# Seven products instead of eight for two token blocks in the second expert chunk, with its token sums and gate steps moved

## The chip, the cores and the metric

The kernel runs on one core of a Trainium2 chip. The metric is device time in microseconds (us), from launch to end, as the median of several executions. The core's engines are TensorE (PE, with its weight loads as PEld), VectorE (DVE), ScalarE (ACT) and GpSimd (POOL); SyncE (SP) issues DMAs. Each engine works through its own queue in order, and semaphores make an instruction wait for others.

## The reference

Three stages follow each other, on 2 x 768 = 1536 tokens of 512 values: windowed attention with 4 sink positions (8 heads of 64), a mixture of 8 experts whose gate is normalized 8 times over rows and columns, and one wide feed-forward layer with a squared ReLU.

```python
x = attention(q, k, v)                      # keep: sink or 0 <= rel < window
logits = x @ w_gate; P = exp(logits - logits.max())
for _ in range(8):
    P /= P.sum(1, keepdims=True) + 1e-09
    P /= P.sum(0, keepdims=True) + 1e-09
    P *= N / E
for e in range(E):
    out += P[:, e:e+1] * (np.maximum(x @ w1[e], 0.0) @ w2[e])
return (np.maximum(out @ w_in, 0.0) ** 2) @ w_out
```

## The kernel before

**Precision and products.** Every float32 operand is kept as two float32r tiles, a rounded high part and the rest (xh and xl, w2h and w2l, hh and hl). ACT writes the high part, and POOL or DVE subtracts it to get the rest. A float32 product is three products on PE: high by rest, high by high, rest by high. `pair_split` (L480 to L482) is the ACT copy and the POOL subtraction of weights and token sums.

**Chunks.** The hidden dimension is cut into chunks of 512: 16 for the experts (two for each expert), 4 for the last layer. Chunk 0 is worked on while attention runs: its groups (`first_groups`) fill PE between attention's steps, in token blocks of 384 (`mm1`, `mm2`). What is left of them when attention ends is drained at the head of `phase_b`, and three second groups of its last block (`rest`) are carried into chunk 1, the second chunk. From chunk 1 on the tokens are in three blocks of 512, numbered 0, 1 and 2.

**First products.** `plain` takes 12 PE products of 512 columns for 128 hidden values of one block. So two blocks need 8 groups, 96 products. The fast chunks (2 to 15, and later 17 to 19) take blocks 0 and 1 together by the seven-product scheme for 2 x 2 blocks: `fast` builds 14 groups of 6 products, 84 in all, for the two halves of the chunk. Each half has five sums out of PSUM on DVE (`tt`, L822), one copy on ACT (L836) and four results, of which each is rounded by ACT and then reduced to hl by DVE (`to_h`, L730 and L740). A set of seven uses four PSUM banks (a, b, c, d); the product p3 writes again to bank c after e5 has read it, p4 to bank d after e7.

**Operands of the scheme.** Weight sums S1 to S4 come from POOL (`unit_sums`, L525, four subtractions of 128x256 per half) and are split by `units`. Token sums T1 to T4 come from `sums` (L671 to L714): differences on DVE (L683) in the scratch tiles x0, x2 and u, then `pair_split`. T1 is written over block B12 of xh and xl (values 0 to 255 of tokens 512 to 1023), so after that block 1 can't be used plain, nor by the gate. T2 to T4 lie in tiles of their own. `sums(0)` is for blocks 0 and 1, with 512 columns, `sums(1)` for the halves of block 2, with 256. Both are planned into chunk 1.

**Second products.** `second` takes 12 products for 128 tokens (L913), and DVE adds the result into acc (`add_up`, L646 in chunk 1). In chunk 2 acc is first scaled by P (L649), from then on every sum is weighted by P (L653).

**The gate.** `gate` (L946) is a generator. Its first three steps are 8 products each (L953, zero-padded gate weights wgz by all tokens of a block) with a copy on ACT; the fourth transposes and takes the maximum per partition; the fifth takes the maximum over partitions (L979) and negates it (L980); the sixth spreads it by a PE product (L983), takes the exponential, and starts the rounds. A round is a PE product with a matrix of ones for the column sums (L1001), a reciprocal and a scaling on DVE (L1005, L1006), and the next row sums, reciprocals, scaling and column sums (L990, L991, L992, L995). P must be ready for chunk 2's sums.

**Order.** It is written out by hand. `run` issues the groups of a list one after the other; behind group k come the steps that `put` has planned for k; and when the running number of the group (from 0 at the head of chunk 1) is in GATE_AT, the next gate step. The PSUM tile of a group is one of 8 banks in turn. DMAs of weights are issued by SP in the order of `load_list`, into three buffers: the fourth is asked for when the first has been used.

Chunk 1 before: one plain group of block 1, three carried-over groups, 7 plain groups of blocks 1 and 0, 4 second groups of block 1, 4 plain groups of block 2, 8 second groups of blocks 0 and 2. The sums for blocks 0 and 1 are behind the groups 0 to 12 of the last 23 of these, those for block 2 behind the groups 15 to 21. The gate's steps begin with the first group and end in chunk 2.

Of the kernel before, what the change touches and what calls it, by code (L numbers as in the profile page):

```python
# [37 lines left out]
NC = NC1 + NC2  # L38
CONV = 3
CONV_AT = (0, 1, 2, 3, 8, 9, 10, 11, 12, 13, 14, 15)  # L40
GATE_AT = (0, 1, 2, 3, 5, 7, 9, 11, 13, 16, 19, 22, 25, 30)
W2_AT = (2, 5, 8, 11)
NB = 512
BIG = 1e30
# [4 lines left out]
class Kernel:  # L49
# [30 lines left out]
    def masks_begin(self):  # L80

        nc, c = self.nc, self.const
        self.raw_nw = self.att.tile([1, 4], I32, name="nw_i")
        for k, src in enumerate((self.nsink, self.window)):
            nc.scalar.dma_start(out=self.raw_nw[:, 2 * k : 2 * k + 2], in_=src.bitcast(I32))
        self.row = self.acc[0:1, NTILE - 1, 0:128]
        nc.vector.memset(self.row, 1.0)
        warm = self.att.tile([128, 1], F32, name="warm")
        nc.vector.memset(warm, 0.0)
        nc.scalar.activation(out=warm, in_=warm, func=AF.Exp)  # L90
        di, ci = self.scratch(0).bitcast(I32), self.scratch(1).bitcast(I32)
        nc.gpsimd.iota(di, pattern=[[-1, 256]], base=128, channel_multiplier=1)
        nc.gpsimd.iota(ci, pattern=[[1, 256]], base=0, channel_multiplier=0)
        nc.vector.tensor_copy(out=self.scratch(2), in_=di)
        self.pm = self.ps_xs.tile([128, 512], F32, tag="xs", name="pm")
        nc.vector.tensor_copy(out=self.pm[:, 256:512], in_=ci)
        nc.vector.tensor_scalar(
            out=self.pm[:, 0:256], in0=self.scratch(2), scalar1=0.0, scalar2=None, op0=ALU.is_lt
        )
        self.ident = c.tile([128, 128], F32, name="ident")  # L100
        make_identity(nc, self.ident)
        a = self.att
        self.junk = a.tile([128, 1], F32, name="junk")
# [332 lines left out]
    def load_list(self, c0):  # L436

        loads, k = [(c0, which, half) for which in range(2) for half in range(2)], 0
        for c in range(c0, NC):
            wide = [(j, 2, 0) for j in range(k, min(k + CONV, 8 * NC2)) if c >= 2]  # L440
            k += len(wide)
            n = c + 1
            loads += wide[0:1]
            if n < NC:
                if self.is_fast(n):
                    loads += [(n, 3, 0), (n, 3, 1)]
                loads += wide[1:2] + [(n, 0, 0)] + wide[2:3] + [(n, 0, 1), (n, 1, 0), (n, 1, 1)]
            else:
                assert len(wide) < 2
        return loads  # L450
# [217 lines left out]
        o = 2 * NB * q + w * t  # L668
        return tuple(x[:, k : k + 2, o : o + w] for x in (self.xh, self.xl))

    def sums(self, q):  # L671

        nc = self.nc
        T = [
            self.tp.tile([128, 3, 2, NB >> q], F32R, tag=f"T{q}{t}", name=f"T{q}{t}")
            for t in "hl"
        ]
        self.T[q] = T

        def tt(o, a, b, op):  # L680
            if isinstance(o, str):
                o = self.scratch2(o)[:, 0 : NB >> q]
            nc.vector.tensor_tensor(out=o, in0=a, in1=b, op=op)  # L683
            return o

        B = {n: self.operand(n, q) for n in ("B11", "B12", "B21", "B22")}
        f32 = lambda n, hl, kc: B[n][hl].bitcast(F32)[:, kc]

        def put(name, kc, x):
            hi, lo = self.operand(name, q)  # L690
            self.pair_split(hi[:, kc], lo[:, kc], x)

        for kc in range(2):
            x = tt("x0", f32("B22", 0, kc), f32("B12", 0, kc), ALU.subtract)
            y = tt("u", f32("B22", 1, kc), f32("B12", 1, kc), ALU.subtract)
            yield
            t3 = tt("x2", x, y, ALU.add)
            put("T3", kc, t3)
            yield
        for kc in range(2):  # L700
            x = tt("x0", f32("B12", 0, kc), f32("B11", 0, kc), ALU.subtract)
            y = tt("u", f32("B12", 1, kc), f32("B11", 1, kc), ALU.subtract)
# [196 lines left out]
    def second(self, c, t):  # L899

        def group(k):
            def go():
# [4 lines left out]
                for i in range(cuts):  # L907
                    d = slice(DM // cuts * i, DM // cuts * (i + 1))
                    ps = self.mmtile()
                    n = 0  # L910
                    for f in (0, 1, 3, 2):
                        for x, w in ((hh, wh), (hh, wl), (hl, wh)):
                            self.nc.tensor.matmul(  # L913
                                out=ps[:, d], lhsT=x[:, f, s], rhs=w[:, f, d], start=(n == 0),
# [127 lines left out]
    def run(self):  # L1042
# [18 lines left out]
        if True:  # L1061
            with tc.manual_schedule():
                first = ExitStack()
                self.wp = self.pool(first, "wp0")
                self.hp0 = self.pool(first, "hp0")
                with ExitStack() as actx:
                    self.wraw = self.pool(actx, "wraw0")
                    self.att = self.pool(actx, "att")
# [124 lines left out]
    def phase_a(self, gen):  # L1193
# [16 lines left out]
        self.att_load_v(1)  # L1210
        for n in (HP - 1, HP):
            self.att_load_qk(n)
        fill = self.filler(gen)
        at = next(fill)
        for u in range(U + 2):
# [56 lines left out]
                self.w_load(0, 1)  # L1272
            if u == 20:
                self.general_flag()
        return fill

    def phase_b(self, c0, first, fill):

# [17 lines left out]
        ]  # L1296
        self.loads, self.lk, self.used = self.load_list(c0), 0, set()
        self.next_loads()
        self.wgz = self.xp_.tile([128, KD, 128], F32R, tag="x0", name="wgz")
        wgr = self.xp_.tile([128, KD, E], F32, tag="x2", name="wgr")  # L1300
        nc.gpsimd.memset(self.wgz.bitcast(F32), 0.0)
        self.ones = self.xp_.tile([128, 128], F32, tag="x1", name="ones")
        nc.gpsimd.memset(self.ones, 1.0)
        nc.sync.dma_start(out=wgr, in_=self.wg)
        todo = [partial(self.units, c0, half, 0, k) for half in range(2) for k in range(2)]
        for _ in fill:
            if self.done:
                self.evac()
                if todo:
                    todo.pop(0)()  # L1310
        self.evac()
        for step in todo:
            step()
        hz = self.wgz[:, :, 0:E]
        nc.scalar.activation(out=hz, in_=wgr, func=AF.Copy)
        nc.vector.tensor_tensor(
            out=self.wgz[:, :, E : 2 * E], in0=wgr, in1=hz.bitcast(F32), op=ALU.subtract
        )
        gate = self.gate()
        groups = itertools.count()  # L1320

        def run(seq, plan):

            for k, g in enumerate(seq):
                g()
                for step in plan.get(k, ()):
                    step()
                if next(groups) in GATE_AT:
                    next(gate, None)

        conv = itertools.chain.from_iterable(self.wide(k) for k in range(8 * NC2))
# [3 lines left out]
        for c in range(c0, NC):  # L1335
# [6 lines left out]

            off = 0
            if not low:
                run([self.plain(c, 1, 0), *rest], {})
                low = first.close() or True
                self.w2p = self.pool(left, "w2" + n)
                self.tp = self.pool(left, "T" + n)
                self.cp, self.T = self.pool(left, "c" + n), {}
                seq = [self.plain(c, t, f) for t in (1, 0) for f in range(KD)][1:]  # L1350
            elif self.is_fast(c):
                seq = self.fast(c, 0, 0) + self.fast(c, 1, 0)
            else:
                seq = [self.plain(c, t, f) for t in (1, 0) for f in range(KD)]
            for k in range(4):
                put(W2_AT[k] if self.is_fast(c) else k, self.part_w2, c, k)
            if c == NC1:
                x = [self.x2(2, kc) for kc in range(KD)]
                seq = sum(([s, *x[k : k + 1]] for k, s in enumerate(seq)), [])
            m = len(seq)  # L1360
            if self.is_fast(c):
                (a, b, *e), (f, g, *i) = (self.fast(c, half, 1) for half in range(2))
                if c < FAST2:
                    seq += self.second(c, 1) + [a, b, f, g]
# [11 lines left out]
            if c == NC1 - 1:  # L1376
# [2 lines left out]
                    ([s, x[k]] for k, s in enumerate(self.second(c, 0) + self.second(c, 2))), []  # L1379
                )  # L1380
                wide = lambda k: m + k if k < 8 else m + 2 * k - 8
            else:
                seq += self.second(c, 0) + self.second(c, 2)
                wide = lambda k: m + k
            if c in (FAST - 1, FAST2 - 1):
                t = self.sums(0)
                for k in range(13):
                    put(k if c < FAST else min(2 * k, k + 5), next, t, None)
                t = self.sums(1)
                for k in range(13):  # L1390
                    put(m + 8 + k // 2, next, t, None)
            if c + 1 < NC:
                if self.is_fast(c + 1):
                    for half in range(2):
# [105 lines left out]
```

## Time and profile before

| | us |
|---|---|
| median of 3 runs (lowest, highest) | 1379.7 (1379.4, 1380.33) |
| the profiled execution's own time | 1379.64 |
| its span, first to last instruction | 1377.8 |
| PE busy in the span | 1363.2 (99%) |
| DVE busy | 955.4 (69%) |
| POOL busy | 501.3 (36%) |
| ACT busy | 453.1 (33%) |

The span is the time from the first to the last instruction; the execution's own time is 1.84 us longer. A share of busy time is a mean over stages that are limited by different engines. The second chunk lies at 181.7 to 247.35 us of the span, behind the fill and the three carried-over groups (from 152 us on).

### The profile page before, as it was taken

What the parts mean: (1) busy time and instruction counts of PE and PEld (TensorE: products, weight loads), DVE (VectorE), ACT (ScalarE), POOL (GpSimd) and SP (SyncE); (2) the same over time, 40 slices, a digit from 0 to 9 for tenths busy, and PEclk for the clock granted to TensorE, in tenths of its full rate; (3) what the DMA queues carried; (4) which work ended last, traced back from release to release, by engine and by line L of the source; (5) the groups of instructions that cost most, each with busy time, mean ns of one, the idle gap of its engine ahead of it and who ended that gap; (6) DMA issues with size and microseconds to landing.
All of it is one profiled execution on the core that took longest, in us unless ns stands there. A gap on an engine that the chain in (4) does not pass through costs nothing.

```text
span 1377.8 us, 18905 instructions
## 1 busy us (share of the span) xinstructions
PE 1363.2 (99%) x7105; PEld 1141.7 (83%) x7105; DVE 955.4 (69%) x1884; ACT 453.1 (33%) x1007; POOL 501.3 (36%) x442
## 2 busy tenths in 40 slices
PE   8999999999999999999999999999999999999998
PEld 5677888888888888888888888888888888888887
DVE  8777369887777777777777768765454568866564
ACT  6776322322232222222232222222232243433331
POOL 4322136524343434424343434423343036543210
PEclk9999999999999999999999999999999999999999
DMA  5222200132313232232313232230102010111101
GB/s 203 81 90 73 78 31 31 62 94 73 124 54 109 79 96 85 92 107 67 118 54 122 70 95 82 92 107 32 61 32 77 16 62 16 62 55 54 46 24 72
DMA packets 61147, 102.53 MB, mean 74 GB/s; under 512 B 3957, under 2 KB 43253, under 8 KB 60789
## 3 DMA queue, kind: packets, MB, share of 16 engines
q1 hardware_dynamic: 61040, 101.22, 23.2%
q8 instruction: 58, 0.95, 0.3%
q14 instruction: 45, 0.36, 0.1%
q10 hardware_dynamic: 4, 0.00, 0.0%
HBM read 89.67 MB, written 11.53 MB: 73 GB/s over the span
## 4 chain that ended last, share of the span: by engine, by line
PE 79%; DVE 1%; ACT 0%; issue 0%; DVEq 0%; ACTq 0%
PE mm L913 42%; PE mm L762 36%; PE mm L930 0%; ACT tx L733 0%; DVE acc L653 0%; DVE tx L734 0%; ACT hh L745 0%; DVE tx L822 0%; DVE hl L746 0%; DVE acc L649 0%; DVE mm L734 0%; DVE raw L578 0%; ACT tx L836 0%; DVE tu L822 0%; DVE raw L565 0%
## 5 line engine op out<-in xcount | busy, mean ns | idle before, releaser
L913 PE MATMUL mm<-w2h,hh 128*128 128x512 f32 (+1 forms) x916 | 357.0, 390 | 0.0
L913 PE MATMUL mm<-w2l,hh 128*128 128x512 f32 (+1 forms) x916 | 355.9, 388 | 0.0
L913 PE MATMUL mm<-w2h,hl 128*128 128x512 f32 (+1 forms) x916 | 355.6, 388 | 0.0
L482 POOL TENSOR_TENSOR w2l<-raw,w2h 128x512 fp32r<-128x512 f32 x76 | 118.5, 1559 | 365.7 <-ACT w2h L481 363.7
L653 DVE SCALAR_TENSOR_TENSOR acc<-mm,P,acc 128x512 f32<-128x512 f32 x168 | 125.7, 748 | 135.6 <-PE mm L913 134.4
L913 PEld LDWEIGHTS mm<-w2h,hl 128*128 128x128 f32 x916 | 172.0, 188 | 35.8
L913 PEld LDWEIGHTS mm<-w2h,hh 128*128 128x128 f32 x916 | 172.1, 188 | 34.6
L913 PEld LDWEIGHTS mm<-w2l,hh 128*128 128x128 f32 x916 | 172.1, 188 | 34.3
L525 POOL TENSOR_TENSOR raw<-raw 128x256 f32<-128x256 f32 x136 | 125.1, 923 | 7.9
L482 POOL TENSOR_TENSOR s0l<-raw,s0h 128x512 fp32r<-128x512 f32 (+1 forms) x36 | 45.5, 1264 | 198.6 <-ACT s0h L481 198.6
L730 ACT ACTIVATE hh<-tx 128x512 fp32r<-128x512 f32 (+1 forms) x112 | 58.8, 525 | 130.0 <-DVE tx L822 129.5
L822 DVE TENSOR_TENSOR tx<-mm,tu 128x512 f32<-128x512 f32 (+1 forms) x136 | 75.6, 556 | 20.9 <-PE mm L762 16.6
L822 DVE TENSOR_TENSOR tx<-mm,tx 128x512 f32<-128x512 f32 (+1 forms) x68 | 37.9, 557 | 57.8 <-PE mm L762 56.5
L740 DVE SCALAR_TENSOR_TENSOR hl<-tx,hh 128x512 fp32r<-128x512 f32 (+1 forms) x112 | 70.1, 626 | 9.7 <-ACT hh L730 9.6
L836 ACT ACTIVATE tx<-mm 128x512 f32<-128x512 f32 x34 | 20.3, 598 | 154.9 <-PE mm L762 153.0
L646 DVE TENSOR_TENSOR acc<-mm,acc 128x512 f32<-128x512 f32 (+1 forms) x49 | 33.2, 677 | 48.2 <-PE mm L913 47.9
L730 ACT ACTIVATE hh<-mm 128x512 fp32r<-128x512 f32 (+1 forms) x68 | 34.0, 501 | 99.2 <-PE mm L762 99.2
L836 ACT ACTIVATE txs<-mm 128x256 f32<-128x256 f32 x34 | 13.0, 381 | 151.3 <-PE mm L762 151.3
L482 POOL TENSOR_TENSOR a0l<-raw,a0h 128x512 fp32r<-128x512 f32 (+1 forms) x38 | 43.0, 1148 | 51.5 <-ACT a0h L481 47.5
L762 PE MATMUL mm<-xl,a1h 128*128 128x512 f32 (+1 forms) x172 | 60.3, 350 | 0.2 <-ACT tx L836 0.2
L762 PE MATMUL mm<-xl,a0h 128*128 128x512 f32 (+1 forms) x172 | 59.8, 348 | 0.0
L762 PE MATMUL mm<-xh,a0h 128*128 128x512 f32 (+1 forms) x172 | 59.8, 347 | 0.0
(262 smaller groups left out, 3149.5 us busy)
## 6 DMA issues: line engine op xcount, KB each, us to landing
raw<-w SPq DMA_DIRECT2D x110, 512.0 KB, 3.7
raw<-win SPq DMA_DIRECT2D x16, 512.0 KB, 4.0
w<-m SPq DMA_DIRECT2D x32, 256.0 KB, 4.6
raw<-wout SPq DMA_DIRECT2D x16, 512.0 KB, 4.0
raw<-qkv SPq DMA_DIRECT2D x8, 624.0 KB, 5.0
raw<-qkv SPq DMA_DIRECT2D x7, 464.0 KB, 3.9
out<-acc SPq DMA_DIRECT2D x11, 256.0 KB, 2.0
wraw<-w SPq DMA_DIRECT2D x2, 1024.0 KB, 6.7
```

The source lines that it names most:

```text
L482: self.nc.gpsimd.tensor_tensor(out=lo, in0=src, in1=hi.bitcast(F32), op=ALU.subtract)
L525: self.nc.gpsimd.tensor_tensor(out=o, in0=x, in1=y, op=op)
L646: nc.vector.tensor_tensor(out=a, in0=ps, in1=a, op=ALU.add)
L653: nc.vector.scalar_tensor_tensor(out=a, in0=ps, scalar=self.P[:, ti, e : e + 1], in1=a, op0=ALU.mult, op1=ALU.add)
L730: nc.scalar.activation(out=hh, in_=src, func=AF.Relu)
L740: nc.vector.scalar_tensor_tensor(out=hl, in0=src, scalar=0.0, in1=hh.bitcast(F32), op0=ALU.max, op1=ALU.subtract,)
L762: self.nc.tensor.matmul(out=ps, lhsT=w[:, kc], rhs=x[:, kc], start=start and k == 0, stop=(k == n - 1), skip_group_check=True,)
L822: nc.vector.tensor_tensor(out=v[name], in0=v[a], in1=v[b], op=ALU.add)
L836: nc.scalar.activation(out=v["s"], in_=v["a"], func=AF.Copy)
L913: self.nc.tensor.matmul(out=ps[:, d], lhsT=x[:, f, s], rhs=w[:, f, d], start=(n == 0), stop=(n == 11),)
```

## The change

Chunk 1 is put into another order. After the fill come one plain group of block 2 and the carried-over groups, then 3 plain groups of block 2, its 4 second groups, 14 groups of the seven-product scheme for blocks 0 and 1, and 8 second groups of blocks 1 and 0. So the token sums for blocks 0 and 1 must be there within chunk 1, and the gate's own products, which read block 1 plain, ahead of T1.

- The gate weights are loaded and split during attention (units 20 and 25), in a pool of their own; the matrix of ones is a constant.
- While the fill drains, the gate's first three steps are issued, then T1, then the weight sums of half 0 and the gate's fourth step.
- T2 to T4 are taken from T1 in another order: all differences of one sum in tiles of their own (u and x1, x0 and x2; T4 in place in T2's), and each sum's `pair_split` is issued later than its differences, behind groups 0 to 6 of the 29.
- The w2 splits of chunk 1 are issued at once behind the carried-over groups.
- Weight sums of half 1 and the S units stand behind groups 2, 3 and 7 to 10; the sums for block 2 behind groups 21 to 27; the preparations for chunk 2 count from group 13.
- The remaining ten gate steps have places of their own in chunk 1.

```diff
-GATE_AT = (0, 1, 2, 3, 5, 7, 9, 11, 13, 16, 19, 22, 25, 30)
+GATE_AT = (
+    (0, 1, 2, 3, 5, 7, 9, 11, 13, 16, 19, 22, 25, 30),
+    (8, 10, 13, 16, 19, 22, 25, 27, 29, 31),
+)
...
+        self.ones = c.tile([128, 128], F32, name="ones")
+        nc.gpsimd.memset(self.ones, 1.0)
...
         loads, k = [(c0, which, half) for which in range(2) for half in range(2)], 0
+        if c0:
+            loads[2:2] = [(c0, 3, 0)]
+            loads.append((c0, 3, 1))
...
+    def sums(self, q, t1_first=False):
...
+        if t1_first:
+            for kc in range(2):
+                x = tt("x0", f32("B12", 0, kc), f32("B11", 0, kc), ALU.subtract)
+                tt(x, x, f32("B12", 1, kc), ALU.add)
+                tt(x, x, f32("B11", 1, kc), ALU.subtract)
+                put("T1", kc, x)
+                yield
+            self.T_tiles(q)
+            jobs = [
+                (n, kc, o, a, b)
+                for n, tags, a, b in (
+                    ("T2", ("u", "x1"), "B22", "B12"), ("T3", ("x0", "x2"), "T2", "B11"),
+                    ("T4", ("u", "x1"), "B21", "T2"),
+                )
+                for kc, o in enumerate(tags)
+            ]
+            t2, made = {}, []
+            for k, (n, kc, o, a, b) in enumerate(jobs):
+                pos = t2[kc] if a == "T2" else f32(a, 0, kc)
+                neg = t2[kc] if b == "T2" else f32(b, 0, kc)
+                x = t2[kc] if n == "T4" else self.scratch2(o)
+                tt(x, pos, neg, ALU.subtract)
+                if a != "T2":
+                    tt(x, x, f32(a, 1, kc), ALU.add)
+                if b != "T2":
+                    tt(x, x, f32(b, 1, kc), ALU.subtract)
+                if n == "T2":
+                    t2[kc] = x
+                made.append((n, kc, x))
+                if k > 1:
+                    put(*made.pop(0))
+                    if k == 3:
+                        put(*made.pop(0))
+                yield
+            for m in made:
+                put(*m)
+            return
...
-                    for f in (0, 1, 3, 2):
+                    for f in (0, 1, 2, 3) if (c, t) == (1, 2) else (0, 1, 3, 2):
...
+            if u in (20, 25):
+                gw.pop(0)()
...
+        gate, early = self.gate(), []
+        if c0:
+            t0 = self.sums(0, True)
+            early = [partial(next, gate)] * 3 + [partial(next, t0)] * 2
+            early += [partial(self.unit_sums, c0, 0, k) for k in range(2)]
+            early.append(partial(next, gate))
+        for at in fill:
             if self.done:
                 self.evac()
                 if todo:
                     todo.pop(0)()
+                if early and (at == NT - QW or len(early) > 5):
+                    early.pop(0)()
...
-                if next(groups) in GATE_AT:
+                if next(groups) in GATE_AT[c0]:
...
-                run([self.plain(c, 1, 0), *rest], {})
+                run([self.plain(c, 1 + c0, 0), *rest], {})
...
+                seq = [self.plain(c, t, f) for t in ((2,) if c0 else (1, 0)) for f in range(KD)]
+                seq = seq[1:]
...
+            mixed = c == c0 == 1
             for k in range(4):
-                put(W2_AT[k] if self.is_fast(c) else k, self.part_w2, c, k)
+                if mixed:
+                    self.part_w2(c, k)
+                else:
+                    put(W2_AT[k] if self.is_fast(c) else k, self.part_w2, c, k)
...
+            if mixed:
+                m += 18
+                put(2, self.finish)
+                seq += self.second(c, 2) + self.fast(c, 0, 0) + self.fast(c, 1, 0)
+                seq += self.second(c, 1)
+                for k in range(2):
+                    put(2 + k, self.units, c, 0, 3, k)
+                    put(7 + k, self.unit_sums, c, 1, k)
+                    put(9 + k, self.units, c, 1, 3, k)
...
+            elif mixed:
+                seq += self.second(c, 0)
+                wide = lambda k: m - 8 + k
...
-                t = self.sums(0)
-                for k in range(13):
-                    put(k if c < FAST else min(2 * k, k + 5), next, t, None)
+                t = t0 if mixed else self.sums(0)
+                for k in range(7 if mixed else 13):
+                    at = (0, 2, 3, 3, 4, 5, 6)[k] if mixed else min(2 * k, k + 5) if c >= FAST else k
+                    put(at, next, t, None)
                 t = self.sums(1)
                 for k in range(13):
-                    put(m + 8 + k // 2, next, t, None)
+                    put(m + (k // 2 if mixed else 8 + k // 2), next, t, None)
```

## Rows read from the trace of the kernel before

**Rows 1.** The page: busy us of each engine, and DVE's 40 slices of 34.4 us.
```profile
PE 1363.2 (99%) x7105; PEld 1141.7 (83%) x7105; DVE 955.4 (69%) x1884; ACT 453.1 (33%) x1007; POOL 501.3 (36%) x442
...
DVE  8777369887777777777777768765454568866564
```

**Rows 2.** The chain of waits: start us, us, engine and line.
```profile
288.59 21.79 PE mm L913 x96
310.38 19.04 PE mm L762 x84
```

**Rows 3.** PE's waits from 150 to 300 us: us in total, times, longest.
```profile
PE mm L762 <- DVE tx L822: 0.6, 1, 0.6
PE mm L1001 <- DVE cs L995: 0.2, 1, 0.2
```

**Rows 4.** Table by stage: the stretch and its us, then busy us of each engine.
```profile
163.60:181.70 18.10, 18.10 (x87) 14.21 (x85) 2.28 (x5) 2.97 (x6) 0.00 (x0) 1.00 0.08 28
181.70:201.86 20.16, 20.16 (x91) 16.32 (x90) 18.18 (x31) 7.61 (x14) 9.32 (x7) 1.00 0.17 53
201.86:225.50 23.64, 23.43 (x106) 19.18 (x105) 22.83 (x39) 6.19 (x11) 14.71 (x15) 1.00 0.00 1
225.50:247.35 21.85, 21.85 (x101) 18.12 (x99) 19.41 (x41) 5.46 (x13) 12.06 (x13) 1.00 0.23 73
```

**Rows 5.** The timeline where the second chunk ends: start us, us, engine, line.
```profile
247.12 0.39 PE L913 MATMUL mm<-w2h,hl 128*128 128x512 f32 x1
...
251.12 0.68 DVE L646 TENSOR_TENSOR acc<-mm,acc 128x512 f32<-128x512 f32 x1
```

**Rows 6.** DVE's timeline in the third chunk, a sum out of PSUM and its follower.
```profile
254.66 0.69 DVE L822 TENSOR_TENSOR tx<-mm,tx 128x512 f32<-128x512 f32 x1 [1.05 <-PE mm L762]
255.27 0.68 DVE L740 SCALAR_TENSOR_TENSOR hl<-mm,hh 128x512 fp32r<-128x512 f32 x1
```

**Rows 7.** DVE's timeline: differences of token sums in the second chunk.
```profile
183.51 0.68 DVE L683 TENSOR_TENSOR tx<-xh 128x512 f32<-128x512 f32 x1
...
186.03 1.79 DVE L683 TENSOR_TENSOR tx<-tx,tu 128x512 f32<-128x512 f32 x1
...
188.75 1.79 DVE L683 TENSOR_TENSOR tx<-xh 128x512 f32<-128x512 f32 x1
190.46 1.78 DVE L683 TENSOR_TENSOR tu<-xl 128x512 f32<-128x512 f32 x1
```

**Rows 8.** POOL's timeline in the same stretch.
```profile
185.99 1.29 POOL L482 TENSOR_TENSOR w2l<-raw,w2h 128x512 fp32r<-128x512 f32 x1 [23.89 <-ACT w2h L481]
188.71 1.29 POOL L482 TENSOR_TENSOR w2l<-raw,w2h 128x512 fp32r<-128x512 f32 x1 [1.43 <-ACT w2h L481]
189.95 1.74 POOL L482 TENSOR_TENSOR T0l<-tx,T0h 128x512 fp32r<-128x512 f32 x1
```

**Rows 9.** Line L683 by stretch: wide differences, then narrow ones; DVE busy us.
```profile
181.70:228.90 47.20, 20.19 (x20) 1.00 0.07 23
228.90:251.70 22.80, 12.43 (x20) 1.00 0.22 70
```

**Rows 10.** Groups on DVE, 181.4 to 251.7: count, busy us, mean ns, idle before.
```profile
L646 DVE TENSOR_TENSOR acc<-mm,acc 128x512 f32<-128x512 f32 x12 | 8.2, 681 | 1.5 <-PE mm L913 1.5
L740 DVE SCALAR_TENSOR_TENSOR hl<-mm,hh 128x512 fp32r<-128x512 f32 x12 | 8.1, 682 | 0.6 <-ACT hh L730 0.6
```

**Rows 11.** PE's timeline: two small products of the gate, the second after a wait.
```profile
192.97 0.38 PE L983 MATMUL mm<-nm,ones 1*128 1x1 f32 x2
...
210.64 0.39 PE L1001 MATMUL mm<-cs,ones 128*128 128x8 f32 x2 [0.21 <-DVE cs L995]
```

**Rows 12.** DVE's timeline: first and last instruction of two gate rounds.
```profile
207.98 0.20 DVE L1005 RECIPROCAL cs<-mm 128x8 f32<-128x8 f32 x1
...
210.25 0.34 DVE L995 TENSOR_REDUCE cs<-P 128x8 f32<-128x104 f32 x1
...
241.23 0.20 DVE L1005 RECIPROCAL cs<-mm 128x8 f32<-128x8 f32 x1
...
242.73 0.35 DVE L995 TENSOR_REDUCE cs<-P 128x8 f32<-128x104 f32 x1
```

More of the change, by code (lines that the diff above doesn't have):

```diff
@@ L669, in operand, with T_tiles @@
         return tuple(x[:, k : k + 2, o : o + w] for x in (self.xh, self.xl))
-    def sums(self, q):
-        nc = self.nc
-        T = [
+    def T_tiles(self, q):
+        self.T[q] = [
             self.tp.tile([128, 3, 2, NB >> q], F32R, tag=f"T{q}{t}", name=f"T{q}{t}")
@@ L677, in sums @@
         ]
-        self.T[q] = T
+    def sums(self, q, t1_first=False):
+        nc = self.nc
         def tt(o, a, b, op):
@@ L691, in put @@
             self.pair_split(hi[:, kc], lo[:, kc], x)
+        if t1_first:
[35 more added lines that the diff above has]
+            return
+        self.T_tiles(q)
         for kc in range(2):
@@ L1065, in run @@
                 self.hp0 = self.pool(first, "hp0")
+                self.gw = self.pool(first, "gw0")
                 with ExitStack() as actx:
@@ L1212, in phase_a @@
             self.att_load_qk(n)
+        gw = list(self.gate_weights(self.gw, ("wgz", "wgr")))
         fill = self.filler(gen)
@@ L1274, in phase_a, with gate_weights, load, split @@
                 self.general_flag()
-        return fill
+            if u in (20, 25):
+                gw.pop(0)()
+        return fill
+    def gate_weights(self, pool, tags):
+        nc = self.nc
+        self.wgz = pool.tile([128, KD, 128], F32R, tag=tags[0], name="wgz")
+        wgr = pool.tile([128, KD, E], F32, tag=tags[1], name="wgr")
+        hz = self.wgz[:, :, 0:E]
+        def load():
+            nc.gpsimd.memset(self.wgz.bitcast(F32), 0.0)
+            nc.sync.dma_start(out=wgr, in_=self.wg)
+        def split():
+            nc.scalar.activation(out=hz, in_=wgr, func=AF.Copy)
+            nc.gpsimd.tensor_tensor(
+                out=self.wgz[:, :, E : 2 * E], in0=wgr, in1=hz.bitcast(F32), op=ALU.subtract
+            )
+        return load, split
     def phase_b(self, c0, first, fill):
@@ L1298, in phase_b @@
         self.next_loads()
[L1299 to L1304, printed above, removed]
-        todo = [partial(self.units, c0, half, 0, k) for half in range(2) for k in range(2)]
-        for _ in fill:
+        if not c0:
+            for step in self.gate_weights(self.xp_, ("x0", "x2")):
+                step()
+        todo = [partial(self.units, c0, half, 0, k) for half in range(2) for k in range(2)]
+        gate, early = self.gate(), []
[5 more added lines that the diff above has]
+        for at in fill:
             if self.done:
@@ L1310, in phase_b @@
                     todo.pop(0)()
+                if early and (at == NT - QW or len(early) > 5):
+                    early.pop(0)()
         self.evac()
-        for step in todo:
+        for step in todo + early:
             step()
[L1314 to L1319, printed above, removed]
         groups = itertools.count()
@@ L1349, in phase_b @@
                 self.cp, self.T = self.pool(left, "c" + n), {}
-                seq = [self.plain(c, t, f) for t in (1, 0) for f in range(KD)][1:]
+                seq = [self.plain(c, t, f) for t in ((2,) if c0 else (1, 0)) for f in range(KD)]
+                seq = seq[1:]
             elif self.is_fast(c):
@@ L1360, in phase_b @@
             m = len(seq)
-            if self.is_fast(c):
+            if mixed:
[7 more added lines that the diff above has]
+                    put(9 + k, self.units, c, 1, 3, k)
+            elif self.is_fast(c):
                 (a, b, *e), (f, g, *i) = (self.fast(c, half, 1) for half in range(2))
```

## The prediction

> **What bounds the kernel now.** I read the busy shares first: TensorE (PE) is busy 1363.2 us of 1377.8, VectorE (DVE) 955.4, and of DVE's slices the seventh (207 to 241 us) alone reaches 9 [rows 1]. In the chain of waits the end hangs on PE alone from 282 us on: 84 products in 19.04 us, 96 in 21.79, so 0.2267 us for one product of 512 columns, every time [rows 2]. So a product that is taken away is worth 0.227 us, if nothing else takes its place. PE's waits between 150 and 300 us are two, 0.6 and 0.2 us [rows 3]. That looks like no trouble, but the table by stage shows how near it is: in the second chunk (181.7 to 247.35) DVE is busy 18.18 of 20.16, 22.83 of 23.64 and 19.41 of 21.85 us, while in the stretch before it (163.6 to 181.7) it does 2.28 of 18.10 [rows 4]. The last sum of that chunk starts on DVE at 251.12, for products of which the last started on PE at 247.12: DVE leaves the chunk about 4 us behind PE [rows 5]. The second chunk is DVE's as much as PE's, and it is the chunk that the change rebuilds.
>
> **The change, part by part.**
>
> *Products.* Blocks 0 and 1 took 8 plain groups of 12 products = 96; two sets of seven take 14 x 6 = 84. 12 x 0.2267 = 2.72 us less on PE. The third block, the second products and the gate's products keep their number. The wait of 0.2 us for the gate's column sums [rows 3] lay in the old order and goes too: -2.9 us together. This is all that the change can give.
>
> *Work added for DVE.* Each half of seven adds five sums out of PSUM (L822, 0.69 us; the instruction behind one starts 0.61 after it [rows 6]): 10 x 0.61 = 6.1 us. The roundings of h stay 12 in number. The token sums stay 20 differences; the six of T1 go forward to the fill, where DVE is nearly idle, for about 6 us. The last gate step (0.5 us) comes in. So DVE's work in the chunk stays about what it was, and its time is 2.7 us shorter.
>
> *Work added for GpSimd (POOL) in the same stretch.* Weight sums of one half (4 subtractions) and the S units of two halves (4 subtractions of 128x512), two of T1 less. This matters because of one thing the timeline shows: a difference of two SBUF tiles takes 0.68 us on DVE when POOL is idle (183.51), and 1.79 when POOL has a subtraction in hand (186.03 against POOL's 185.99; 188.75; 190.46): it ends about 0.5 us after POOL's does [rows 7, 8]. POOL pays as well: 1.74 instead of 1.29 [rows 8]. Over the 20 wide differences the mean is 20.19 / 20 = 1.01 us, over the narrow ones 12.43 / 20 = 0.62 [rows 9]. Operations with an input in PSUM are not touched: 12 of L646 mean 681 ns, 12 of L740 682 ns [rows 10].
>
> The Trainium skill says of this (SBUF — State Buffer, "Who interferes with whom") that a VectorE instruction with two SBUF inputs and a GpSimd instruction that reads SBUF exclude each other, and that the later one blocks for the whole of the other. The trace's 1.79 us is less than the 0.68 + 1.29 = 1.97 us of a full block, since the wait overlaps the start-up. At 1.97 each of the five held differences of stretch A below would cost 0.2 us more, 1 us in all.
>
> *Fill and early steps.* The gate's three product sets move before the fill's groups; they cost PE the same there. T1's second half waits for its scratch tile x0, which POOL still reads for the first half, and ACT's copy for T1 stands ahead of ACT's copy for the last h slice, as does DVE's difference; the last f step of the first carried-over group needs that slice. Cover: the plain group in between and 9 products, 2.72 + 2.04 = 4.8 us, against two chains of three differences (2.0 alone, 3.4 held) and their copies. Between 0 and 1.2 us; I take 0.5. The loads and sums that are issued early stand behind idle queues: POOL has 0.00 us in that stretch [rows 4]. One load (the first weight sums) takes the place of another in the first three, nothing. The gate weights' memset, load and split move into attention, one instruction each on POOL, SP, ACT and POOL: nothing, at most a wait like the two of [rows 3], 0.2 to 0.6. The w2 splits, issued at once, are counted in stretch A.
>
> *Stretch A: from the end of the carried-over groups to the product with the negated maximum (L983).* It stands after seven groups in PE's queue, 7 x 2.72 = 19.0 us, and PE cannot pass it. DVE must do before it: a copy and one rounding 1.2; three differences of T2 against POOL's four w2l subtractions, 1.6 each: 6.0; two roundings: 7.2; then the rounding of the third plain group, which `finish` puts ahead of T2's other half, and which waits for PE (8.2) and ACT (0.6): 9.5; then nine differences (T2 three, T3 four, T4 two) 9 x 0.62 = 5.6, two sums into acc 1.2, the maximum 0.4: 16.7 with POOL idle, 2.3 early. But POOL is given six subtractions in that time (two S units, two T2, two T3), each 1.1 us to a difference behind it: 23.3, 4.3 late. At the corresponding place of before four differences stood against five subtractions, and the three in [rows 7] from 186.03 on were all held. I take five of six held: 22.2, so a **wait of 3.2 us** (0 to 4.3). The change thereby makes late a step that was not: before, that product came after four groups, with T3's differences alone ahead of the maximum on DVE, and started without a wait at 192.97 [rows 11].
>
> *Stretch B: the fourteen groups of six.* PE: 14 x 1.36 = 19.0, the product itself 0.6, four rounds' products at about 0.2: 20.5. DVE from the maximum on: two sums 1.2; T4's other half 1.9; bias and exponential 1.2; five gate rounds (1.85 alone, 241.23 to 243.08, 2.6 held by POOL, 207.98 to 210.59 [rows 12]) 9.3; ten L822 6.5 (half of them wait for the one before); seven of the eight roundings 4.6, of which those out of scratch tiles meet POOL's weight sums: 1.3 more. 26.0. DVE may trail PE by about two products (the fourth bank of a set is written again one product later), so 5.5 - 2.6 = **2.9 us** (0 to 4.5).
>
> *Stretch C: the eight second groups.* PE 8 x 2.72 + 0.7 = 22.5. DVE: 8 sums 4.9, 20 narrow differences 20 x 0.54 = 11, one rounding, three rounds 5.8, the last step 0.5: 23. That alone would be hidden, as it was before, when three groups lay between rounds. Now the rounds stand at every second group: two groups are 5.4 + 0.2 on PE, and 1.2 + 3.4 + 1.9 = 6.5 on DVE, and each round's product waits for the column sums of the round before, as it did once for 0.21 us (210.64 [rows 11]). Three pairs x 0.9, less the first one's slack: **2.0 us** (0 to 3.0). In return DVE enters the third chunk less behind than the 4 us of before; that lag cost nothing there, so nothing comes back.
>
> Sum: -2.9 + 0.5 + 3.2 + 2.9 + 2.0 = +5.7. On the profiled execution's own 1379.64 us that is 1385.3; the median of the runs is 0.06 above it, so 1385.4.
>
> **The rivals.**
> *PE alone decides (faster).* Every new wait stays hidden: POOL finds other moments, stretch A is 2.3 early as counted. 1379.7 - 2.9 = 1376.8. Its place is stretch A, and it decides from the point where no more than two of the nine late differences there are held (16.7 + 2.2 = 18.9 against 19.0); DVE then enters B on time. For it: PE's 99%, and a kernel whose waits are 0.8 us over this whole region. Against it: DVE at 97% of 201.86 to 225.5 before 6 us more are put in, and the held differences. The Trainium skill's rule to work first on the engine with the highest occupancy (Perfetto Trace Analysis, "Identifying the Most-Contended Engine") would by PE's share say this; the same page warns that busy time misjudges PE, and that the engine can change from stretch to stretch.
> *One wait only.* The gate's wait in A comes, and PE's delay lets DVE catch up, so B and C stay hidden: -2.9 + 3.2 = 1380.0, no difference. For it: B and C had bounds that begin at 0. Against it: the rounds follow each other at fixed groups, and DVE starts B behind.
> *Everything held (slower still).* Upper ends of all: 1.2 + 4.3 + 4.5 + 3.0 - 2.9 = +10.1: 1389.8. It decides if POOL's queue is full through all three stretches.
> *The change does not do what it says.* If the T or S operands come later than the products (the second product of a set needs T2 and S2), the sevens wait for POOL. In stretch A's count T2's second half leaves DVE at about 15 us, some 5 us before that product. It would cost 1 to 2 us, is within the bounds of A, and has no chance of its own.
>
> **How the numbers follow.** Forecast (waits of 4 to 9 us) 0.54: 1382.5 to 1387.5. PE alone 0.21, one wait only 0.16, everything held 0.09. A measurement of this kernel tells about 0.2% (2.8 us) from no change. PE alone lands at 2.9 us, right at that bound, so I split it: 0.13 faster, 0.08 same. One wait only is same, with 0.01 of the forecast: same 0.25. Slower: the rest of the forecast and the last rival, 0.53 + 0.09 = 0.62. The range takes in PE alone, 1376.6, and nearly all held, 1388.5.
>
> **What would show it.** Right: 12 products fewer in the second chunk; a wait of PE for DVE's maximum (L979/L980) at the product L983 of 2 to 4 us near 200 us; several waits of about 1 us at L1001 for L995; T differences of 1.7 us; the last products of the chunk starting some 5 us later than before, all else after it the same. Wrong: no wait of PE above 0.5 us between 165 and 260, or DVE idle in the fourteen groups of six; then the answer is 1376.8. If A's wait is there but the rounds start at once, it is the second rival.

## The result and the profile after

The changed kernel takes 1387.2 us, the median of 4 runs (1385.06 to 1387.7), against 1379.7 before. The ratio of the two sets of runs is 1.0051, with a 95% interval of 1.0039 to 1.0063. It is slower by about 7.5 us. Its profiled execution took 1386.88 us with a span of 1385.1; before it was 1379.64 with 1377.8. So the spans differ by 7.3 us, and that is what the trace has to account for.

The page of the kernel after: busy us of each engine, and DVE's 40 slices.
```profile
PE 1364.7 (99%) x7093; PEld 1141.6 (82%) x7093; DVE 964.5 (70%) x1893; ACT 456.9 (33%) x1013; POOL 514.8 (37%) x455
...
DVE  8777378787777777686777777775464567866564
```
PE has 12 instructions fewer than in [rows 1], and 1.5 us *more* busy time. Busy time of PE should have fallen by 2.7, so some products got slower. The share of 99% is the same as before: it shows nothing of the loss.

The chain of waits of the kernel after: start us, us, engine and line.
```profile
296.40 21.79 PE mm L960 x96
318.19 19.04 PE mm L809 x84
```
These are the two groups of [rows 2], with the same durations, 7.81 us later. From here to the end the distance shrinks by 0.5 us in all (the spans differ by 7.3), so the loss arises before 296 us.

PE's waits of the kernel after from 140 to 300 us: us in total, times, longest.
```profile
PE mm L1030 <- DVE nm L1027: 3.5, 1, 3.5
PE mm L1048 <- DVE cs L1042: 2.4, 2, 1.5
PE mm L809 <- DVE tx L869: 0.8, 2, 0.6
PE mm L809 <- ACT tx L883: 0.2, 1, 0.2
```
Against [rows 3] (0.6 and 0.2) there are now 6.9 us. L1030 is the product with the negated maximum (L983 before), L1048 that of a gate round (L1001 before), L809 a first product and L869 a sum out of PSUM (L822 before). Every wait but 0.2 is for DVE.

PE's timeline of the kernel after, around the waits and behind them: start us, us, engine, line, and in brackets the idle time before it.
```profile
201.33 0.39 PE L960 MATMUL mm<-w2h,hl 128*128 128x512 f32 x1
205.19 0.58 PE L1030 MATMUL mm<-nm,ones 1*128 1x1 f32 x2 [3.47 <-DVE nm L1027]
205.70 0.80 PE L809 MATMUL mm<-xl,a0h 128*128 128x512 f32 x1
206.29 0.63 PE L809 MATMUL mm<-xh,a0h 128*128 128x512 f32 x1
206.72 0.63 PE L809 MATMUL mm<-xh,a0l 128*128 128x512 f32 x1
...
211.58 0.39 PE L809 MATMUL mm<-xh,s0l 128*128 128x512 f32 x1
211.81 0.40 PE L809 MATMUL mm<-xl,s0h 128*128 128x512 f32 x1
...
244.82 0.39 PE L1048 MATMUL mm<-cs,ones 128*128 128x8 f32 x2 [0.87 <-DVE cs L1042]
...
252.31 0.39 PE L1048 MATMUL mm<-cs,ones 128*128 128x8 f32 x2 [1.51 <-DVE cs L1042]
...
255.40 0.39 PE L809 MATMUL mm<-xl,a0h 128*128 128x512 f32 x1
```
Two things stand here. The product that started without a wait in [rows 11] is now 3.47 us late. And behind it products of 512 columns start 0.43 us apart (206.29, 206.72), not 0.23 as at 211.58 and 211.81. The last row is the start of the third chunk: 255.40, where it was 247.35 before, 8.05 us later.

The table by stage of the kernel after: the stretch and its us, then busy us of PE, PEld, DVE, ACT and POOL, PE's granted clock, DMA share and GB/s.
```profile
182.30:201.70 19.40, 19.40 (x87) 15.65 (x85) 17.19 (x17) 7.06 (x13) 13.56 (x9) 1.00 0.25 82
201.70:205.20 3.50, 0.03 (x2) 0.01 (x1) 3.43 (x6) 0.78 (x2) 2.52 (x2) 0.89 0.00 0
205.20:208.00 2.80, 2.80 (x7) 2.33 (x8) 2.77 (x4) 0.23 (x1) 1.27 (x1) 0.50 0.00 0
208.00:211.00 3.00, 3.00 (x9) 2.35 (x8) 2.02 (x7) 1.49 (x3) 2.13 (x3) 0.50 0.00 0
211.00:214.00 3.00, 3.00 (x15) 2.54 (x14) 1.92 (x5) 0.63 (x1) 2.10 (x4) 0.96 0.00 0
```
While PE waits (second row), DVE is busy for 3.43 of 3.50 us. Then the granted clock is 0.50, the lower of its two levels (1.2 and 2.4 GHz), for 5.8 us, with PE busy all the time; before, it was 1.00 throughout [rows 4]. Twelve products at 0.427 instead of 0.2267 us apart are **2.4 us that are no wait in any list**. They are the larger part of the 4.2 us of busy time that the page has too much (1.5 more, where 2.7 less were due).

DVE's timeline of the kernel after in the stretch that makes PE wait.
```profile
188.47 1.27 DVE L787 SCALAR_TENSOR_TENSOR hl<-mm,hh 128x512 fp32r<-128x512 f32 x2
191.38 0.69 DVE L787 SCALAR_TENSOR_TENSOR hl<-mm,hh 128x512 fp32r<-128x512 f32 x1 [1.64 <-ACT hh L777]
191.99 1.80 DVE L692 TENSOR_TENSOR tx<-xh 128x512 f32<-128x512 f32 x1
193.83 3.36 DVE L692 TENSOR_TENSOR tx<-tx,xl 128x512 f32<-128x512 f32 x2
...
197.71 0.68 DVE L692 TENSOR_TENSOR tx<-tu,xh 128x512 f32<-128x512 f32 x1
198.43 1.66 DVE L692 TENSOR_TENSOR tx<-tx,xl 128x512 f32<-128x512 f32 x1
...
203.13 1.63 DVE L692 TENSOR_TENSOR tu<-tu,xl 128x512 f32<-128x512 f32 x1
204.69 0.27 DVE L1026 TENSOR_REDUCE nm<-mm 1x1 f32<-1x128 f32 x1
204.99 0.14 DVE L1027 TENSOR_SCALAR nm<-nm 1x1 f32<-1x1 f32 x1
```
POOL's timeline of the kernel after in the same stretch.
```profile
183.30 6.39 POOL L490 TENSOR_TENSOR w2l<-raw,w2h 128x512 fp32r<-128x512 f32 x4 [3.09 <-ACT w2h L489]
191.95 3.00 POOL L490 TENSOR_TENSOR s0l<-raw,s0h 128x512 fp32r<-128x512 f32 x2 [2.25 <-ACT s0h L489]
194.90 1.74 POOL L490 TENSOR_TENSOR T0l<-tu,T0h 128x512 fp32r<-128x512 f32 x1
197.93 1.60 POOL L490 TENSOR_TENSOR T0l<-tx,T0h 128x512 fp32r<-128x512 f32 x1 [1.29 <-ACT T0h L489]
200.83 3.39 POOL L490 TENSOR_TENSOR T0l<-tx,T0h 128x512 fp32r<-128x512 f32 x2 [1.29 <-ACT T0h L489]
```
Of the three differences from 191.99 on the first takes 1.80 us and the next two 1.68 each, against POOL's three subtractions; the one at 197.71 takes 0.68, as POOL is idle when it starts; the next, at 198.43, meets POOL's subtraction of 197.93 and takes 1.66. It is the pattern of [rows 7, 8], and it is in front of the maximum now.

### The profile page after: what moved, and what is told of

It is laid out like the page before. It is cut to its first block, busy times and chain, and to the rows that moved or that the text cites. A ratio compares the mean times of both kernels' runs of the same rounds, so it can differ in the third digit from the quotient of the medians.

```text
span 1385.1 us, 18921 instructions
## 1 busy us (share of the span) xinstructions
PE 1364.7 (99%) x7093; PEld 1141.6 (82%) x7093; DVE 964.5 (70%) x1893; ACT 456.9 (33%) x1013; POOL 514.8 (37%) x455
## 4 chain that ended last, share of the span: by engine, by line
PE 79%; DVE 0%; issue 0%; DVEq 0%
PE mm L960 42%; PE mm L809 37%; PE mm L977 0%; DVE acc L661 0%; DVE acc L657 0%; DVE raw L586 0%; DVE tx L869 0%; DVE tu L869 0%; DVE raw L573 0%; DVE acc L654 0%; DVE raw L578 0%; DVE raw L582 0%; DVEq L661 0%; DVE m L590 0%; DVEq L869 0%
## 5 line engine op out<-in xcount | busy, mean ns | idle before, releaser
L533 POOL TENSOR_TENSOR raw<-raw 128x256 f32<-128x256 f32 x144 | 130.5, 910 | 10.4 <-DMA raw<-w 1.2
L490 POOL TENSOR_TENSOR s0l<-raw,s0h 128x512 fp32r<-128x512 f32 (+1 forms) x38 | 48.8, 1287 | 206.5 <-ACT s0h L489 195.7
L869 DVE TENSOR_TENSOR tx<-mm,tu 128x512 f32<-128x512 f32 (+1 forms) x140 | 78.4, 560 | 22.2 <-PE mm L809 18.1
L787 DVE SCALAR_TENSOR_TENSOR hl<-tx,hh 128x512 fp32r<-128x512 f32 (+1 forms) x116 | 73.7, 635 | 10.0 <-ACT hh L777 9.9
L869 DVE TENSOR_TENSOR tx<-mm,tx 128x512 f32<-128x512 f32 (+1 forms) x70 | 39.3, 561 | 59.1 <-PE mm L809 57.7
L883 ACT ACTIVATE tx<-mm 128x512 f32<-128x512 f32 x36 | 21.5, 598 | 157.2 <-PE mm L809 154.9
L490 POOL TENSOR_TENSOR a1l<-raw,a1h 128x512 fp32r<-128x512 f32 (+1 forms) x38 | 40.4, 1082 | 59.6 <-ACT a1h L489 59.6
L787 DVE SCALAR_TENSOR_TENSOR hl<-tu,hh 128x512 fp32r<-128x512 f32 (+1 forms) x58 | 60.1, 1037 | 1.4
L777 ACT ACTIVATE hh<-mm 128x512 fp32r<-128x512 f32 (+1 forms) x62 | 30.6, 493 | 88.9 <-PE mm L809 88.9
L210 POOL TENSOR_TENSOR qkl<-raw,qkh 128x672 fp32r<-128x672 f32 (+3 forms) x24 | 33.4, 1412 | 67.7 <-ACT qkh L209 59.8
```

The source lines that it names most:

```text
L210: nc.gpsimd.tensor_tensor(out=cut(lo), in0=cut(raw), in1=cut(hi.bitcast(F32)), op=ALU.subtract)
L490: self.nc.gpsimd.tensor_tensor(out=lo, in0=src, in1=hi.bitcast(F32), op=ALU.subtract)
L533: self.nc.gpsimd.tensor_tensor(out=o, in0=x, in1=y, op=op)
L777: nc.scalar.activation(out=hh, in_=src, func=AF.Relu)
L787: nc.vector.scalar_tensor_tensor(out=hl, in0=src, scalar=0.0, in1=hh.bitcast(F32), op0=ALU.max, op1=ALU.subtract,)
L869: nc.vector.tensor_tensor(out=v[name], in0=v[a], in1=v[b], op=ALU.add)
```

## The experiments

**Theory:** DVE is late for the gate, because the token sums T2 to T4 stand ahead of the maximum and POOL's subtractions hold them (first place), and because the rounds stand at every second group in the last eight (second place). The clock falls as a result of the first wait. **Rivals:** the lag belongs to the order of seven products itself and only moves when a cause is taken away; or the clock, not the wait, is the main loss. The runs of before beside these had medians of 1379.83 and 1379.84.

**1. The differences of T2 ahead of the carried-over groups**, in x1 and x2; T3 takes x0 and u. The numbers of instructions stay.
```diff
-                    ("T2", ("u", "x1"), "B22", "B12"), ("T3", ("x0", "x2"), "T2", "B11"),
-                    ("T4", ("u", "x1"), "B21", "T2"),
+                    ("T2", ("x1", "x2"), "B22", "B12"), ("T3", ("x0", "u"), "T2", "B11"),
+                    ("T4", ("x1", "x2"), "B21", "T2"),
...
-            early.append(partial(next, gate))
+            early += [partial(next, gate)] + [partial(next, t0)] * 2
...
-                for k in range(7 if mixed else 13):
-                    at = (0, 2, 3, 3, 4, 5, 6)[k] if mixed else min(2 * k, k + 5) if c >= FAST else k
+                for k in range(5 if mixed else 13):
+                    at = (0, 1, 2, 4, 5)[k] if mixed else min(2 * k, k + 5) if c >= FAST else k
```


> The six T2 differences move ahead of the carried-over groups, where DVE has idle time and POOL little to do (scratch tiles x1 and x2 instead of u and x1, T3 in x0 and u). Theory (DVE is late at the negated maximum because its differences are held by POOL's subtractions): the maximum is ready about 5 us sooner, PE's wait of 3.47 us at the product with it falls under 0.5, the granted clock stays at 1.00 after 205 us, and the T2 differences take 0.7 us each. The rounds in the fourteen short groups then wait up to 1.5 us in all, because PE no longer gives DVE time; the two waits of 0.87 and 1.51 us in the second groups stay. 1382 us (1381 to 1383.5). Rival (PE waits because the gate's steps stand too close, whatever DVE does before them): the wait stays above 2 us and the time within 1 us of 1387.2.

Measured: 1380.63 us, 1.0008 (0.9999 to 1.0017) times before, and 6.6 under after. PE's waits in this run, 150 to 300 us:
```profile
PE mm L1049 <- DVE cs L1043: 2.4, 2, 1.5
PE mm L810 <- DVE tx L870: 0.8, 2, 0.6
PE mm L810 <- ACT tx L884: 0.2, 1, 0.2
```
The wait for the maximum is gone, the granted clock is 1.00 in every stretch, and the waits for the rounds have not moved by 0.1 us. 3.5 of wait and 2.4 of clock make 5.9 of the 6.6; most of the rest lies in the two starts right behind the wait, 0.51 and 0.59 us apart in after (205.19, 205.70, 206.29) and 0.30 and 0.34 here. The expectation was 1.4 us too high, with its whole range (1381 to 1383.5): it left room for more waits in the groups of six, and there were 0.43.

**2. PE kept busy in the wait.** 15 products whose result nobody reads, ahead of the product with the maximum, into its own PSUM tile.
```diff
         ps = self.mmtile()
+        for _ in range(15):
+            nc.tensor.matmul(
+                out=ps, lhsT=self.xh[:, 2, 0:128], rhs=self.xh[:, 2, 0:512], start=True, stop=True
+            )
         nc.tensor.matmul(out=ps[:, 0:1], lhsT=self.ones[0:1, :], rhs=nm, start=True, stop=True)
```


> Fifteen products whose result nobody reads (3.4 us at 0.2267 each) stand ahead of the product with the negated maximum, so PE works while DVE finishes the maximum; nothing else is changed. Theory (the wait itself costs 3.5 us, and the granted clock of 0.50 that follows it costs 12 products 0.2 us more each, 2.4 us, but this time DVE uses to catch up): the clock stays at 1.00, the fourteen short groups get back waits of 1 to 2 us at the rounds, and the time falls by 0.5 to 1.5 us: 1386 us. Rival (the clock is lost time in full): 2.4 us less, 1384.8, and no new wait. Second rival (the clock does not depend on the wait): the clock falls again and the time stays at 1387.

Measured: 1385.92 us, 1.0044 (1.0031 to 1.0058). A stretch of its table by stage, and its waits of 150 to 300 us:
```profile
205.20:208.00 2.80, 2.67 (x13) 2.01 (x12) 2.73 (x6) 0.63 (x1) 1.29 (x1) 1.00 0.00 0
```
```profile
PE mm L1052 <- DVE cs L1046: 3.3, 4, 1.5
PE mm L809 <- DVE tx L869: 0.8, 2, 0.6
PE mm L809 <- ACT tx L883: 0.3, 1, 0.3
```
With products in the gap the clock stays at 1.00: it was the gap that let it fall. But the kernel wins 1.3 us by the medians, not 2.4. This gain is not clear of the scatter (the two intervals overlap), but the traces give the same picture: the third chunk starts 1.0 us earlier than in after (254.40 against 255.40). Two waits for the rounds more have come, 0.77 and 0.15 us in the groups of six. In after, DVE caught up by that much while PE ran at half speed. So the clock is not the main loss; and here a slower PE hid a late DVE.

**3. POOL without reads.** Eleven subtractions on POOL (the w2 parts, the S units of half 0, T2, T3 and the first half of T4) become memsets to zero, so these low parts are zeros in the products.
```diff
+        if self.blank:
+            self.nc.gpsimd.memset(lo.bitcast(F32), 0.0)
+            return
         self.nc.gpsimd.tensor_tensor(out=lo, in0=src, in1=hi.bitcast(F32), op=ALU.subtract)
```


> Eleven of POOL's subtractions between the carried-over groups and the seventh group behind them (four of w2, two of the S units, five of T2 to T4) are left out: POOL sets those rest parts to zero instead, so it writes as many tiles but reads none. DVE's instructions and their order are the same. Theory (POOL's subtractions hold DVE's differences of two SBUF tiles): the fourteen differences of T2 to T4 take about 0.7 us each instead of 1.4 in the mean, the wait of 3.47 us at the negated maximum is gone, the clock stays at 1.00, 1381.5 to 1383 us. Rival (DVE has simply too many instructions there): the differences get no shorter by more than a fifth and the wait stays above 2 us, 1386 or more.

Measured: 1380.81 us, 1.0007 (0.9997 to 1.0016). DVE's timeline in this run, and POOL's:
```profile
185.19 1.42 DVE L695 TENSOR_TENSOR tu<-tu,xl 128x512 f32<-128x512 f32 x2
...
192.66 0.68 DVE L695 TENSOR_TENSOR tx<-xh 128x512 f32<-128x512 f32 x1
193.38 1.49 DVE L695 TENSOR_TENSOR tx<-tx,xl 128x512 f32<-128x512 f32 x2
...
198.64 0.68 DVE L695 TENSOR_TENSOR tu<-xh,tu 128x512 f32<-128x512 f32 x1
```
```profile
183.29 1.94 POOL L491 MEMSET w2l<- 128x512 f32 x4 [2.41 <-PE mm L640]
185.17 1.00 POOL L491 MEMSET s0l<- 128x512 f32 x2
186.11 2.40 POOL L491 MEMSET T0l<- 128x512 f32 x5
```
All fourteen differences take 0.67 to 0.75 us, the product with the maximum doesn't wait, and the time is that of experiment 1 within 0.2 us, 0.7 under the expected range. The same order, with as many instructions in the same places, has no first wait if POOL does not read: the cause is the holding, not the amount of DVE's work. The rival of the order as such falls for this place. The memsets are also shorter than the subtractions (0.48 against 1.6 us each), but a difference beside them is not held at all: the two from 185.19 on take 1.42 us together, while POOL is in memsets from 183.29 to 188.51. (The eleven from 192.66 on run with POOL idle.) The Trainium skill (SBUF — State Buffer, "Who interferes with whom") says as much: a DVE instruction with two SBUF inputs contends with a POOL instruction that reads SBUF, not with one that only writes it. The trace agrees, with these 1.42 us.

**4. Only the last three gate places later**, behind groups 28, 31 and 34.
```diff
-    (8, 10, 13, 16, 19, 22, 25, 27, 29, 31),
+    (8, 10, 13, 16, 19, 22, 25, 28, 31, 34),
```


> Only the last three gate steps move: from behind groups 27, 29 and 31 to behind 28, 31 and 34 (the last one in the third chunk), so that rounds stand at every third of the second groups as in the kernel before. Theory (rounds at every second group make PE wait for column sums): the waits of 0.87 and 1.51 us go, PE enters the third chunk 2 to 3 us sooner, but DVE is no sooner done, so up to 2 us come back as one wait at the last round in the third chunk: 1385.5 us (1384.5 to 1387). Rival (those waits are all of it and nothing comes back): 1384.8. The wait at the negated maximum and the clock after it stay as they are in both.

Measured: 1386.58 us, 1.0051 (1.0037 to 1.0064); 0.6 under after, which is within the scatter. PE's timeline in this run:
```profile
257.15 0.39 PE L1048 MATMUL mm<-cs,ones 128*128 128x8 f32 x2 [1.98 <-DVE cs L1042]
```
The two waits in the last eight groups (2.38) are gone, and one of 1.98 stands where the third chunk begins. Here the rival that a lag only moves is right, as this run's expectation had it: the lag was handed on, since DVE has next to no idle time there (busy 1.86 of the 2.00 us from 255 to 257). Moving a consumer is worth something only if DVE catches up before it.

**5. Both, with all gate places spread:** the edit of experiment 1, and the steps two to four groups apart, but for the last, which stands six further on, in the third chunk.
```diff
-    (8, 10, 13, 16, 19, 22, 25, 27, 29, 31),
+    (6, 10, 13, 17, 20, 22, 25, 28, 31, 37),
```


> The T2 differences ahead of the carried-over groups, as in the run that moved them alone, and the ten later gate steps spread: behind groups 6, 10, 13, 17, 20, 22, 25, 28, 31 and 37, so rounds stand at every third of the second groups and the last step in the third chunk. Theory (the twelve products saved are worth 2.72 us as soon as DVE is not late anywhere): the waits of 0.87 and 1.51 us at the rounds go, and with DVE early in stretch A nothing comes back in the third chunk but about 1 us at one round: 1378.0 us, 1.5 to 2.5 us under the kernel before. Rival (the lag only moves on, as when the gate steps were moved alone, where a wait of 1.98 us stood in the third chunk): 1380 or more, no faster than the run with T2 moved alone.

Measured: **1376.99 us**, 0.9981 (0.9972 to 0.999) times before: 2.85 us faster than before, and 10.2 than after. Its waits of 150 to 300 us:
```profile
PE mm L810 <- DVE tx L870: 0.6, 1, 0.6
PE mm L1049 <- DVE cs L1043: 0.4, 1, 0.4
```
They are 1.0 us, before had 0.8 [rows 3]; the expectation, 1378.0, was 1.0 too high and had 1 us of wait at one round, where there were 0.4. So the time saved is that of the 12 products, 2.72 us, within the scatter. What the change removes is real; all that hid it was the place of DVE's work.

**6. The spread gate places alone**, without the early T2 (the last diff on the kernel after).

> The changed kernel with the spread gate steps alone (6, 10, 13, 17, 20, 22, 25, 28, 31, 37), T2 where the change puts it. Theory (DVE is late behind its held differences, and the gate step is only the first thing on PE that shows it): the wait at the negated maximum goes, since that step now stands ahead of most T differences, but 4 to 5 us of wait appear at the next round's product near 211 us, and the clock falls behind it as before; the waits in the second groups shrink: 1384 us (1383 to 1386). Rival (the wait belongs to the step with the maximum): no wait above 1 us anywhere, 1381 or less.

Measured: 1383.64 us, 1.003 (1.002 to 1.0041); 3.6 under after. PE's waits of 150 to 300 us, the longest of them in PE's timeline, and two stretches of the table by stage:
```profile
PE mm L1048 <- DVE cs L1042: 4.6, 2, 4.3
PE mm L809 <- DVE tx L869: 0.6, 1, 0.6
```
```profile
210.61 0.39 PE L1048 MATMUL mm<-cs,ones 128*128 128x8 f32 x2 [4.25 <-DVE cs L1042]
```
```profile
210.00:212.00 2.00, 1.39 (x6) 1.20 (x7) 1.86 (x5) 0.00 (x0) 1.84 (x4) 0.84 0.00 0
212.00:214.00 2.00, 2.00 (x7) 1.52 (x6) 1.57 (x6) 0.77 (x2) 1.18 (x3) 0.50 0.00 0
```
The maximum is taken two groups earlier on DVE, ahead of eight of the fourteen differences, and its product waits no more; the wait has gone to the first round, with 4.25 us, and the clock falls there. In both orders the held differences make PE wait at the gate's next product behind them. The two edits come out as the table says, in us against after:

| | rounds as in after | rounds spread |
|---|---|---|
| T2 late | 0 | -3.6 |
| T2 early | -6.6 | -10.2 |

They add up within the scatter, so neither edit takes away what the other takes. Of what the spread wins alone, the last three places are worth 0.6 at most (experiment 4); which of its other places wins the rest was not tried.

## Why the prediction was right, and where its terms were off

The forecast was 1385.4 us and slower; 1387.2 was measured. By the profiled execution, +5.7 was forecast and +7.2 measured.

- *Products, -2.72.* Right: 7105 to 7093, and experiment 5 gets that time.
- *Fill and early steps, 0.5.* No wait is listed there. The chunk's run starts at 182.39 instead of 181.70, 0.7 later, of which 0.1 was there before 150 us: 0.6.
- *Stretch A, 3.2.* Measured 3.47. Place, product and cause are those of the prediction. Of the nine differences behind the third rounding five were taken as held; six were, one of them for half (1.16). The prediction's reason for the price, a wait that overlaps the start-up, was only argued: the rows show that a held difference ends some 0.5 us after POOL's subtraction, where a free one takes 0.68.
- *What failed in A is what it left out:* behind this wait PE's products ran at the lower clock. That is 2.4 us of PE's time, of which experiment 2 gives back 1.3 by the medians.
- *Stretch B, 2.9.* Measured 0.42, two waits of 0.21. With the clock kept up (experiment 2) they are 0.77, 0.27, 0.15 and 0.21: 1.4, so the term was mis-sized even without the clock. It was not DVE's part: in experiment 2 DVE takes 25.6 us from the maximum to the end of its seventh rounding (205.50 to 231.07), where 26.0 were counted, and ends 2.5 us behind the last of the groups of six, where 2.6 were allowed. PE's part was too short: 205.63 to 228.54 are 22.9 us, without the 1.4 of waits 21.5, where 20.5 were counted. The price of the held roundings was right: three out of scratch tiles take 1.12 to 1.22 us where a free one takes 0.68, 1.5 more for the three, where 1.3 was taken.
- *Stretch C, 2.0.* Measured 0.87 and 1.51, so 2.38, at the forecast product. A pair of groups was taken as 6.5 us on DVE. From one column sum to the next, 244.43 to 251.92, it was 7.5, with DVE never idle: the seven differences in it took 4.6 us where 3.4 were counted, since POOL holds narrow ones too (0.96 instead of 0.41). That DVE leaves the chunk less behind was right: its last sum starts at 256.50, the last product at 255.17, so 1.3 us where it was 4 [rows 5].
- *The sum.* -2.9 + 0.6 + 3.47 + 2.4 + 0.42 + 2.38 = 6.4, where the trace has 8.05 at the start of the third chunk. Of the remaining 1.6 about 0.5 are the two starts right behind the first wait (experiment 1). The rest was not taken apart by a run; it may be the gate's small products and the starts behind the other waits. In experiment 5, without these waits, the third chunk starts at 244.87, 2.5 us before that of before. Before the end 0.7 of the 8.05 come back.

Of the rivals, *PE alone decides* gives its 1376.8 in experiment 5 (1376.99), once the differences of T2 stand earlier and the rounds further apart: it was right about the gain, wrong about this order. Its point (two of nine held) was passed by far, with six. *One wait only* would have been 1380.0; the waits in C say no. *Everything held* (1389.8) was further off than the forecast, and its large terms were not there.

So the forecast's total was held up by two errors of opposite sign: B by 2.5 too much, the clock and the small gaps by 4.0 too little. The step that makes PE wait was foreseen; that the total came so near is in part luck.

## What to carry to other kernels

A wait in PE's queue is set by what stands ahead of its producer on the producer's queue; count that, with the price that operations have beside their neighbours (here 1.7 instead of 0.68 us), before you take products away. Where two edits each move a late consumer, run them alone and together: one that only moves the lag shows it at the next consumer. And look at busy time against the number of instructions: here fewer products and more busy time were the sign of a lower clock, which no list of waits has and the table by stage shows.

## What the runs showed of the hardware

- After 3.47 us in which PE had no product (after; 3.48 in experiment 4) the granted clock was 0.50 for about 6 us, with PE busy all the time, and then 1.00 again. It had fallen at about 204.4 in after, while PE still waited. After a wait of 4.25 us (experiment 6) it fell only when PE had been busy again for some 0.6 us, and was back sooner: PE's products start 0.24 us apart just before 211.41, 0.43 apart from there to 214.40, then 0.23. After waits of 1.51 and 1.98 us it did not fall:
```profile
252.40:255.00 2.60, 2.60 (x13) 2.17 (x14) 2.43 (x5) 0.42 (x1) 0.74 (x1) 1.00 0.28 93
```
  This is the stretch of after right behind its wait of 1.51. Why the lower level lasts differently long was not tried. Of after's four runs three have a mean clock of 0.996 and 1386.88 us or more, and one has 0.999 and 1385.06, near experiment 2's time.
- A difference on DVE that POOL's subtraction holds takes 1.63 to 1.80 us instead of 0.68, the narrow ones (256 columns) 0.96 instead of 0.41; POOL's own takes 1.6 to 1.74 instead of 1.29. A rounding whose input is in PSUM is not held: the two from 188.47 on take 1.27 us together, beside POOL's four subtractions that run from 183.30 to 189.69. One out of a scratch tile is (1.05 to 1.22 in the groups of six of after).
